# Causal attention and MLP: four heads at a time in 32-row and 32-column TensorE tiles, turns on VectorE, and one list schedule for all engines

## The chip, the core and the metric

The kernel runs on one core of a Trainium2 chip. The metric is device microseconds of one execution, here 478.67 (median of 3, 476.93 to 481.06). The profile of one execution spans 474.5 us from its first to its last instruction.

The engines are named as in the profile: PE (TensorE, matrix products), PEld (its weight loads), DVE (VectorE), ACT (ScalarE), POOL (GpSimd), SP (SyncE, which here only starts transfers).

## The reference

Attention over 8 batches of 8 heads, 576 queries of width 64, with 16 "beacon" keys ahead of 576 causal ones; then an MLP with a gated activation over all 4608 tokens.

```python
B, H, S, Nb, D = (8, 8, 576, 16, 64)
k_all = np.concatenate([beacon_k, k], axis=2)
v_all = np.concatenate([beacon_v, v], axis=2)
scores = scale * np.matmul(q, k_all.transpose(0, 1, 3, 2))      # scale = 1/8
causal[:, Nb:] = np.triu(np.ones((S, S), dtype=bool), k=1)
scores = np.where(causal, -1000000000.0, scores)
scores = scores - scores.max(-1, keepdims=True)
a = np.exp(scores)
a /= a.sum(-1, keepdims=True) + 1e-09
attn = np.matmul(a, v_all)
# ---- MLP, d_model 512, d_ff 2048 ----
x = attn.transpose(0, 2, 1, 3).reshape(B * S, H * D)
h = x @ w_in
g = h * (1.0 / (1.0 + np.exp(-1.702 * h)))
return (g @ w_out).astype(np.float32)
```

All inputs and the output are float32; both kernels multiply in float16.

## The kernel before

Attention goes by head pairs: 32 steps of two heads (NPAIR = 4 pairs a batch). q and k are loaded with the token on the partition, and turned by TensorE against an identity, then copied out of PSUM by ScalarE (q) and VectorE (k):

```python
def tr_pair(b, p, which):
    ...
        for i in range(NSB):                       # NSB = 5 row blocks; batch 0 has a form of its own
            rows = min(P, S - i * P)
            nc.tensor.transpose(
                u[:, i * P : i * P + rows],
                src[0:rows, i, 2 * p : 2 * p + 2, :].rearrange("r h d -> r (h d)"),
                ident[0:rows, 0:rows],
            )
    ...
    if which == 0:
        nc.scalar.copy(out=dst, in_=srcv)
    else:
        nc.vector.tensor_copy(out=dst, in_=srcv)
```

Scores are made with keys on the partition, in four chunks a pair, each head in one 64-row half of the array; exp goes from PSUM to SBUF, and the diagonal blocks are masked by VectorE (first 8 pairs) or GpSimd:

```python
def qk_chunk(i, ci):
    ...
    sc = pss.tile([P, 2, 512], F32, tag="s", name="s")          # pss: 2 buffers
    for (j, a, e) in CH[ci]:
        for x in range(2):
            r = 64 * x
            nc.tensor.matmul(sc[:, x, o : o + e - a],
                kT[r : r + 64, p, j * P : (j + 1) * P], qT[r : r + 64, p, a:e], start=True, stop=True)
    nc.scalar.activation(out=E[...], in_=sc[:, :, 0:o], func=AFT.Exp, scale=0.125)
    ...                                                          # mask of diagonal blocks
```

Values carry 64 columns of ones beside the 64 of v, so that the sums come out of the same matmul. The result is copied to SBUF; the sums are gathered by DMA, inverted, sent to DRAM and spread back over the partitions; GpSimd multiplies:

```python
def av_half(i, x, half):
    u = psu.tile([P, HS], F32, tag="u", name="u")                # psu: 3 buffers
    ...  nc.tensor.matmul(u[:, lo - qa : hi - qa], lhs, E[0:kw, x, col : col + hi - lo], ...)
    nc.vector.tensor_copy(out=O[:, p % 2, qa:qe], in_=u[:, :])

def z_gather(b, hf):   # SP: zc <- O, two transfers
def z_recip(b, hf):    # DVE: rc = 1 / zc;  SP: zd (DRAM) <- rc;  SP: rz <- zd, broadcast over 64 rows
def norm(b, hf):       # POOL: xT = O * rz, four multiplies of [64, 576]
```

The MLP goes in nine groups of 512 tokens. The first layer's four matmuls fill a bank, ScalarE makes the tanh and VectorE the gate; the second layer collects 16 matmuls in one bank (pso: 1 buffer), which ScalarE copies out:

```python
def mlp1(g, nt):
    u = psu.tile([P, GT], F32, tag="u", name="u")
    ...  nc.tensor.matmul(u[:, o : o + w], w1t[:, kp, nt * P : (nt + 1) * P], xT[:, kp, m : m + w], ...)
    nc.scalar.activation(out=sig[:, :], in_=u[:, :], func=AFT.Tanh, scale=0.851)
    nc.vector.scalar_tensor_tensor(out=gts[g][:, nt, :], in0=sig[:, :], scalar=1.0, in1=u[:, :],
                                   op0=ALU.add, op1=ALU.mult)

def mlp2(g, mt, qt):
    for nt in range(4 * qt, 4 * qt + 4):
        nc.tensor.matmul(o[:, :], gts[g][:, nt, mt * P : (mt + 1) * P], w2t[:, nt, :], ...)
    if qt == 3:
        nc.scalar.mul(out=osb[:, :], in_=o[:, :], mul=0.5)
        nc.sync.dma_start(out=out[t0 : t0 + P, :], in_=osb[:, :])
```

The order is fixed by hand: each step's attention pieces are spread over the step, and up to eight MLP pieces (`QUOTA = 8`) are put between them. A group of the MLP is begun when the whole batches that it needs are normalised. Loads start in the order: q and k of two head pairs at a time, v, then w1, then batch 1.

Of the kernel before, what the change touches and what calls it, by code (L numbers as in the profile page):

```python
# [11 lines left out]
ALU = mybir.AluOpType  # L13


@with_exitstack
def kernel(
# [19 lines left out]
    P = 128  # L37
    NJ = (NK + P - 1) // P
    NSB = (S + P - 1) // P
    NKPAD = NJ * P  # L40
    NPAIR = H // 2
    NKP = DMODEL // P
    NNT = DFF // P
    TR = 6
    TP = S // TR
    HS = S // 2
    GT = 512
    NG = NTOK // GT
    RING = 4
    NSTEP = B * NPAIR  # L50
    QUOTA = 8
    LAG = 6
# [4 lines left out]
    ld = ctx.enter_context(tc.tile_pool(name="ld", bufs=2))  # L57
    tp = ctx.enter_context(tc.tile_pool(name="tp", bufs=2))
    ep = ctx.enter_context(tc.tile_pool(name="ep", bufs=2))
    op_ = ctx.enter_context(tc.tile_pool(name="op", bufs=2))  # L60
# [3 lines left out]
    pss = ctx.enter_context(tc.tile_pool(name="pss", bufs=2, space=bass.MemoryType.PSUM))  # L64
    psu = ctx.enter_context(tc.tile_pool(name="psu", bufs=3, space=bass.MemoryType.PSUM))
    pso = ctx.enter_context(tc.tile_pool(name="pso", bufs=1, space=bass.MemoryType.PSUM))
    dr = ctx.enter_context(tc.tile_pool(name="dr", bufs=4, space=bass.MemoryType.DRAM))


    ident = cst.tile([P, P], F16, tag="ident", name="ident")  # L70
    make_identity(nc, ident)

    keep = cst.tile([P, P + Nb], F16, tag="keep", name="keep")
# [7 lines left out]
        pattern=[[1, P + Nb]],  # L81
        channel_multiplier=-1,
    )
    w1t = cst.tile([P, NKP, DFF], F16, tag="w1", name="w1")
    w2t = cst.tile([P, NNT, DMODEL], F16, tag="w2", name="w2")
    xT = cst.tile([P, NKP, RING * S], F16, tag="xT", name="xT")

    vbs = [cst.tile([P, NJ, H, 2 * D], F16, tag=f"vb{i}", name=f"vb{i}") for i in range(2)]
    for t in vbs:
        nc.vector.memset(t[:, :, :, D : 2 * D], 1.0)  # L90


    nat = {}

    def new_nat(b):

        shape = [TP, H, TR * D] if b == 0 else [P, NSB, H, D]
        qn = ld.tile(shape, F16, tag="qn", name="qn")
        kn = ld.tile(shape, F16, tag="kn", name="kn")
        bk = ld.tile([Nb, H, D], F16, tag="bk", name="bk")  # L100
        nat[b] = (qn, kn, bk)

    def load_qk(b, h0, h1):
        qn, kn, _ = nat[b]
        for t, src in ((qn, q), (kn, k)):
            if b == 0:
                nc.gpsimd.dma_start(
                    out=t[:, h0:h1, :],
                    in_=src[b, h0:h1].rearrange("h (p t) d -> p h (t d)", t=TR),
                )  # L110
                continue
            for i in range(NSB):
                rows = min(P, S - i * P)
                nc.gpsimd.dma_start(  # L114
                    out=t[0:rows, i, h0:h1, :],
                    in_=src[b, h0:h1, i * P : i * P + rows, :].rearrange("h s d -> s h d"),
                )

    def load_bk(b):
        nc.gpsimd.dma_start(out=nat[b][2][:, :, :], in_=beacon_k[b].rearrange("h n d -> n h d"))  # L120

    def load_v(b, j, h0, h1):
        vb = vbs[b % 2]
        if j == 0:
            nc.gpsimd.dma_start(
                out=vb[0:Nb, 0, h0:h1, 0:D],
                in_=beacon_v[b, h0:h1].rearrange("h n d -> n h d"),
            )
            nc.gpsimd.dma_start(
                out=vb[Nb:P, 0, h0:h1, 0:D],  # L130
                in_=v[b, h0:h1, 0 : P - Nb, :].rearrange("h n d -> n h d"),
            )
        else:
            lo = j * P - Nb
            hi = min(lo + P, S)
            nc.gpsimd.dma_start(  # L136
                out=vb[0 : hi - lo, j, h0:h1, 0:D],
                in_=v[b, h0:h1, lo:hi, :].rearrange("h n d -> n h d"),
            )

    def load_w1(c):
        w = DFF // 4
        nc.gpsimd.dma_start(
            out=w1t[:, :, c * w : (c + 1) * w],
            in_=moe_w_in[:, c * w : (c + 1) * w].rearrange("(a p) n -> p a n", p=P),
        )

    def load_w2(c):
        n = NNT // 4
        nc.gpsimd.dma_start(  # L150
            out=w2t[:, c * n : (c + 1) * n, :],
            in_=moe_w_out[c * n * P : (c + 1) * n * P, :].rearrange("(a p) n -> p a n", p=P),
        )


    qk = {}

    def new_qk(b):
        qT = tp.tile([P, NPAIR, S], F16, tag="qT", name="qT")
        kT = tp.tile([P, NPAIR, NKPAD], F16, tag="kT", name="kT")  # L160
        nc.gpsimd.memset(kT[:, :, NK:NKPAD], 0.0)
        qk[b] = (qT, kT)

    def tr_beacon(b):
        bk, kT = nat[b][2], qk[b][1]
        u = psu.tile([P, NPAIR, Nb], F16, tag="u", name="u")
        for p in range(NPAIR):
            nc.tensor.transpose(u[:, p, :], bk[:, 2 * p : 2 * p + 2, :], ident[0:Nb, 0:Nb])  # L168
        nc.vector.tensor_copy(out=kT[:, :, 0:Nb], in_=u[:, :, :])

    def tr_pair(b, p, which):
        src = nat[b][which]
        dst = qk[b][0][:, p, :] if which == 0 else qk[b][1][:, p, Nb:NK]
        if b == 0:
            u = psu.tile([P, TR, TP], F16, tag="u", name="u")
            for t in range(TR):
                for x in range(2):
                    nc.tensor.transpose(
                        u[64 * x : 64 * x + 64, t, :],
                        src[:, 2 * p + x, t * D : (t + 1) * D],  # L180
                        ident[0:TP, 0:TP],
                    )
            dst = dst.rearrange("r (p t) -> r p t", t=TR)
            srcv = u[:, :, :].rearrange("r t p -> r p t")
        else:
            u = psu.tile([P, S], F16, tag="u", name="u")
            for i in range(NSB):
                rows = min(P, S - i * P)
                nc.tensor.transpose(  # L189
                    u[:, i * P : i * P + rows],  # L190
                    src[0:rows, i, 2 * p : 2 * p + 2, :].rearrange("r h d -> r (h d)"),
                    ident[0:rows, 0:rows],
                )
            srcv = u[:, :]
        if which == 0:
            nc.scalar.copy(out=dst, in_=srcv)  # L196
        else:
            nc.vector.tensor_copy(out=dst, in_=srcv)  # L198


    s0s = [max(0, j * P - Nb) for j in range(NJ)]


    CH = [
        [(0, 0, 512)],
        [(0, 512, S), (2, s0s[2], S), (4, s0s[4], S)],
        [(1, s0s[1], S)],
        [(3, s0s[3], S)],
    ]
    ecol = {}  # L210
    choff = []
    c0 = 0
    for ch in CH:
        choff.append(c0)
        for (j, a, e) in ch:
            ecol[(j, a)] = c0
            c0 += e - a
    ETOT = c0
    Es = {}

    def e_pieces(j, a, e):

        got = []
        for (jj, qa), col in ecol.items():
            if jj != j:
                continue
            qe = qa + [x[2] - x[1] for ch in CH for x in ch if x[0] == jj and x[1] == qa][0]
            lo, hi = max(a, qa), min(e, qe)
            if lo < hi:
                got.append((lo, hi, col + lo - qa))  # L230
        return got

    def qk_chunk(i, ci):
        b, p = divmod(i, NPAIR)
        qT, kT = qk[b]
        if ci == 0:
            Es[i] = ep.tile([P, 2, ETOT], F16, tag="E", name="E")
        E = Es[i]
        sc = pss.tile([P, 2, 512], F32, tag="s", name="s")
        o = 0  # L240
        for (j, a, e) in CH[ci]:
            for x in range(2):
                r = 64 * x
                nc.tensor.matmul(  # L244
                    sc[:, x, o : o + e - a],
                    kT[r : r + 64, p, j * P : (j + 1) * P],
                    qT[r : r + 64, p, a:e],
                    start=True,
                    stop=True,
                )  # L250
            o += e - a
        nc.scalar.activation(  # L252
            out=E[:, :, choff[ci] : choff[ci] + o],
            in_=sc[:, :, 0:o],
# [3 lines left out]
        for (j, a, e) in CH[ci]:  # L258
            if a != s0s[j]:
                continue  # L260
            w = P - Nb if j == 0 else min(P, S - a)
            mc = Nb if j == 0 else 0
            col = ecol[(j, a)]
            blk = E[:, :, col : col + w]
            if i < 8:
                for x in range(2):
                    nc.vector.tensor_tensor(  # L267
# [178 lines left out]
    for p in range(NPAIR):  # L446
        load_qk(0, 2 * p, 2 * p + 2)
        if p == 0:
            load_bk(0)
# [102 lines left out]
```

The softmax here doesn't subtract the row's maximum and nothing guards it: scores larger than these inputs give would overflow.

## Time and profile before

| what | value |
|---|---|
| time | 478.67 us |
| span in the profile | 474.5 us |
| mean granted TensorE clock | 0.941 |
| first matmul of the MLP's first layer (line 382) | 89.8 us |
| last score matmul (line 244) | 378.8 us |
| small packets (under 512 B) | 109696 of 122016 |

The profile gives busy time and share of the span for each engine, and then the span in 40 equal slices of 11.9 us, with one digit for the busy tenths of each. Matmuls are pipelined, so that the mean duration of one is longer than the distance from one to the next. A line such as `L382 PE MATMUL u<-xT,w 128*128 128x512 f16 x512 | busy, mean | idle <- releaser` names the line of the kernel, the engine and operation, what is written and read, rows and columns of the array, the moving operand, the count, the busy microseconds, the mean nanoseconds of one, and the idle time of the engine just before, with what ended it. In the chain of waits, one goes back from the last instruction to what released it, step by step.

### The profile page before, as it was taken

How to read it: one execution, taken by the hardware profiler on the slowest of the kernel's cores; microseconds unless marked ns; L12 is line 12 of the kernel's file. 1: busy time of each engine (PE TensorE's matmuls, PEld its weight loads, DVE VectorE, ACT ScalarE, POOL GpSimd, SP SyncE). 2: the span in 40 equal slices, each digit the busy share in tenths (PEclk: the TensorE clock that was granted, in tenths of full speed). 3: DMA queues.
4: the chain of work that ended last, by engine and by line, in shares of the span. 5: the costliest groups of instructions: out<-in, count | busy, mean ns of one | idle time of the engine just before them, and what ended most of it. 6: DMA issues, size and time to landing. Idle time of an engine off the chain costs nothing.

```text
span 474.5 us, 6853 instructions
## 1 busy us (share of the span) xinstructions
PE 396.0 (83%) x2584; PEld 201.8 (43%) x2584; DVE 193.0 (41%) x410; ACT 222.8 (47%) x341; POOL 251.3 (53%) x348
## 2 busy tenths in 40 slices
PE   2505555889999999899989998999899999899985
PEld 1303333444444444444444456645444444444432
DVE  5403373755125522561256226622561373184410
ACT  3303433665456545664466446644665442263421
POOL 9945078489528952895379627954616250400000
PEclk9955675899999999999999999999999999999999
DMA  9999939959614981399129911990203112100111
GB/s 86 157 176 179 82 46 148 79 44 111 111 59 56 111 122 46 65 107 129 47 55 110 134 48 52 108 140 34 63 2 95 56 42 64 77 1 22 46 44 66
DMA packets 122016, 38.22 MB, mean 81 GB/s; under 512 B 109696, under 2 KB 115328, under 8 KB 121984
## 3 DMA queue, kind: packets, MB, share of 16 engines
q0 software_dynamic: 111424, 18.62, 54.9%
q1 hardware_dynamic: 10560, 19.18, 14.2%
q8 instruction: 20, 0.33, 0.3%
q14 instruction: 12, 0.10, 0.1%
HBM read 46.66 MB, written 9.58 MB: 119 GB/s over the span
## 4 chain that ended last, share of the span: by engine, by line
PE 59%; ACT 17%; POOL 7%; DMA 7%; DVE 5%; issue 4%; ACTq 0%; POOLq 0%; DVEq 0%
PE o L408 26%; PE u L382 19%; ACT E L252 8%; PE u L310 6%; ACT sig L391 5%; PE u L189 4%; DVE g L392 4%; PE s L244 3%; ACT osb L417 3%; DMA w<-in_moe_w_in_dram 3%; DMA bk<-in_beacon_k_dram 2%; POOL kn L114 1%; POOL vb L136 1%; DMA zc<-O 1%; POOL xT L354 1%
## 5 line engine op out<-in xcount | busy, mean ns | idle before, releaser
L382 PE MATMUL u<-xT,w 128*128 128x512 f16 (+1 forms) x640 | 144.7, 358 | 12.5 <-DVE g L392 12.4
L408 PE MATMUL o<-w,g 128*128 128x512 f16 x576 | 144.1, 379 | 9.7 <-ACT osb L417 9.7
L392 DVE SCALAR_TENSOR_TENSOR g<-sig,u 128x512 f16<-128x512 f16 x144 | 99.0, 687 | 104.9 <-ACT sig L391 104.8
L354 POOL TENSOR_TENSOR xT<-O,rz 64x576 f16<-64x576 f32 x64 | 89.6, 1400 | 79.9 <-DMA rz<-zd 76.3
L391 ACT ACTIVATE sig<-u 128x512 f16<-128x512 f32 x144 | 87.6, 609 | 77.3 <-PE u L382 72.9
L252 ACT ACTIVATE E<-s 128x1024 f16<-128x1024 f32 (+3 forms) x128 | 104.7, 876 | 14.8 <-PE s L244 8.8
L317 DVE COPY O<-u 128x288 f32<-128x288 f32 x128 | 56.3, 453 | 71.2 <-PE u L310 69.9
L382 PEld LDWEIGHTS <-w 128*128 128x128 f16 x640 | 56.8, 97 | 63.3 <-issue 20.4
L274 POOL TENSOR_SCALAR_AFFINE_SELECT E<-E 128x256 f16<-128x256 f16 (+2 forms) x120 | 43.1, 395 | 67.0 <-ACT E L252 66.3
L408 PEld LDWEIGHTS <-g 128*128 128x128 f16 x576 | 50.2, 97 | 63.1 <-issue 15.6
L310 PE MATMUL u<-E,vb 128*128 128x288 f16 (+6 forms) x576 | 69.5, 260 | 5.3 <-DVE O L317 5.1
L310 PEld LDWEIGHTS <-vb 128*128 128x128 f16 (+1 forms) x576 | 52.5, 104 | 36.8 <-issue 12.2
L417 ACT ACTIVATE osb<-o 128x512 f32<-128x512 f32 x36 | 21.5, 597 | 82.1 <-PE o L408 82.1
L244 PE MATMUL s<-qT,kT 64*128 64x80 f16 (+5 forms) x384 | 44.1, 307 | 18.4 <-ACT E L252 9.9
L196 ACT COPY qT<-u 128x576 f16<-128x576 f16 x32 | 20.5, 640 | 73.4 <-PE u L189 66.7
L244 PEld LDWEIGHTS <-kT 64*128 64x128 f16 x384 | 17.1, 99 | 58.6 <-issue 46.2
L114 POOL DMA_DIRECT2D kn<-in_k_dram x35 | 29.6, 883 | 5.9 <-DMA w<-in_moe_w_in_dram 5.9
L136 POOL DMA_DIRECT2D vb<-in_v_dram x36 | 29.7, 860 | 2.7 <-DMA w<-in_moe_w_out_dram 2.7
L198 DVE COPY kT<-u 128x576 f16<-128x576 f16 x32 | 15.7, 492 | 37.2 <-PE u L189 35.6
L114 POOL DMA_DIRECT2D qn<-in_q_dram x35 | 29.9, 884 | 0.0
L168 PE MATMUL u<-ident,bk 16*128 16x16 f16 x32 | 2.1, 170 | 28.2 <-DMA bk<-in_beacon_k_dram 28.2
L267 DVE TENSOR_TENSOR E<-E,keep 128x128 f16<-128x128 f16 (+2 forms) x80 | 17.1, 271 | 14.0 <-ACT E L252 13.6
(29 smaller groups left out, 108.8 us busy)
## 6 DMA issues: line engine op xcount, KB each, us to landing
rz<-zd SPq DMA_DIRECT2D x32, 288.0 KB, 4.4
out_dram<-osb SPq DMA_DIRECT2D x36, 256.0 KB, 2.0
qn<-in_q_dram POOLq DMA_DIRECT2D x28, 128.0 KB, 4.2
kn<-in_k_dram POOLq DMA_DIRECT2D x28, 128.0 KB, 4.4
vb<-in_v_dram POOLq DMA_DIRECT2D x21, 128.0 KB, 6.0
w<-in_moe_w_in_dram POOLq DMA_DIRECT2D x4, 512.0 KB, 9.3
w<-in_moe_w_out_dram POOLq DMA_DIRECT2D x4, 512.0 KB, 9.5
vb<-in_v_dram POOLq DMA_DIRECT2D x7, 112.0 KB, 3.3
```

Source lines behind the costliest of these rows:

```text
L114: nc.gpsimd.dma_start(out=t[0:rows, i, h0:h1, :], in_=src[b, h0:h1, i * P : i * P + rows, :].rearrange("h s d -> s h d"),)
L244: nc.tensor.matmul(sc[:, x, o : o + e - a], kT[r : r + 64, p, j * P : (j + 1) * P], qT[r : r + 64, p, a:e], start=True, stop=True,)
L252: nc.scalar.activation(out=E[:, :, choff[ci] : choff[ci] + o], in_=sc[:, :, 0:o], func=AFT.Exp, scale=0.125,)
L274: nc.gpsimd.affine_select(out=blk, in_=blk, compare_op=ALU.is_ge, fill=0.0, base=mc, pattern=[[0, 2], [1, w]], channel_multiplier=-1,)
L310: nc.tensor.matmul(u[:, lo - qa : hi - qa], lhs, E[0:kw, x, col : col + hi - lo], start=(n == 0), stop=(n == len(mm) - 1),)
L317: nc.vector.tensor_copy(out=O[:, p % 2, qa:qe], in_=u[:, :])
L354: nc.gpsimd.tensor_tensor(out=xT[r : r + 64, p, c : c + S], in0=O[r : r + 64, a, :], in1=rz[r : r + 64, a, :], op=ALU.mult,)
L382: nc.tensor.matmul(u[:, o : o + w], w1t[:, kp, nt * P : (nt + 1) * P], xT[:, kp, m : m + w], start=(kp == 0), stop=(kp == NKP - 1),)
L391: nc.scalar.activation(out=sig[:, :], in_=u[:, :], func=AFT.Tanh, scale=0.851)
L392: nc.vector.scalar_tensor_tensor(out=gts[g][:, nt, :], in0=sig[:, :], scalar=1.0, in1=u[:, :], op0=ALU.add, op1=ALU.mult,)
L408: nc.tensor.matmul(o[:, :], gts[g][:, nt, mt * P : (mt + 1) * P], w2t[:, nt, :], start=(nt == 0), stop=(nt == NNT - 1),)
L417: nc.scalar.mul(out=osb[:, :], in_=o[:, :], mul=0.5)
```

## The change

The new kernel takes four heads (a "set") at a time, 16 sets in all, and replaces several parts:

- **Turning q and k.** They are loaded so that partition 32h + r holds 18 tokens of head h in one run. VectorE transposes 32 x 32 squares of four-byte words; a word is two neighbouring float16 values of a row. So partition 32h + c holds elements 2c and 2c+1 of head h, and the two are taken apart by a step of two in the matmul's operands. No transposes on TensorE are left.
- **Scores.** Each head has 32 rows of the array, four heads side by side, in two passes (`d` = 0, 1) that add up. One score buffer of four banks in place of two buffers of two.
- **Values and sums.** Four heads side by side in 32 columns each; three groups: the lower and the upper half of v's columns, and ones.
- **Normalisation.** VectorE alone: transpose of the sums, reciprocal of one column, transpose back over 32 columns, and one multiply out of PSUM into `xT`, which now holds all tokens.
- **PSUM.** Values, first layer and second layer share a ring of four single banks.
- **Order.** A list schedule made when the program is built: every operation has an engine, an assumed length and its dependencies, and the order on all engines is that of the starts in this plan. Attention of later sets is held to due times from 30 to 275 us of the plan.
- **Groups.** Tokens 0 to 511 make two groups of 256; a group needs only the half batches that it covers.
- **Loads.** w1 comes in 24 pieces (its rows follow the new order of `xT`'s partitions), after q and k of two sets and v of batch 0; w2 after them.

The diff, cut to its core:

```diff
-    QUOTA = 8
-    LAG = 6
+class Plan:
+    LAT = {"PE": 230, "ACT": 60, "DVE": 60, "POOL": 60, "Q": 1900, "SP": 0}
+    ...                                    # list schedule, one queue for each engine
+    def choose(self, ok, t, mode, last, free):
+        ...                                # scores first; values late or in the same tile mode; then m1 and m2 in turn
@@ loads and turns
-            t = ld.tile([P, NSB, H, D]) ...  src[b, h0:h1, i * P : i * P + rows, :].rearrange("h s d -> s h d")
+            out=dst[s % NB3][:, :],
+            in_=src[b, Q * hs : Q * hs + Q].rearrange("h (r t) d -> (h r) (t d)", t=TR),
-                nc.tensor.transpose(u[:, ...], src[...], ident[0:rows, 0:rows])
-            nc.scalar.copy(out=dst, in_=srcv)
-            nc.vector.tensor_copy(out=dst, in_=srcv)
+        nc.vector.transpose(
+            out=f32(dst.rearrange("p n e -> p (n e)")).rearrange("p (r t) -> p t r", t=TR),
+            in_=f32(src[:, :]).rearrange("p (t c) -> p t c", t=TR),
+        )
@@ scores
-    pss = ... bufs=2 ...  sc = pss.tile([P, 2, 512], F32)
+    pss = ... bufs=1 ...  sc = pss.tile([P, Q, 512], F32)
+    CH = [
+        [(0, 0, HF), (1, s0s[1], HF), (2, s0s[2], HF)],
+        [(0, HF, S), (4, s0s[4], S)],
+        [(2, HF, S), (3, s0s[3], s0s[4])],
+        [(3, s0s[4], S), (1, HF, S)],
+    ]
+            for d in range(2):
+                for h in range(Q):
+                    r = 32 * h
+                    nc.tensor.matmul(
+                        sc[:, h, o : o + e - a],
+                        kT[s % NB2][r : r + 32, j * P : (j + 1) * P, d],
+                        qT[s % NB2][r : r + 32, a:e, d],
+                        start=(d == 0),
+                        stop=(d == 1),
+                    )
@@ values and sums
+    def e_av(s, x, half):
+        u = ring_tile(("av", s, x, half))
+            for h in range(Q):
+                lhs = ones[0:kw, :] if x == 2 else vb[...][0:kw, j, Q * hs + h, HD * x : HD * x + HD]
+                nc.tensor.matmul(u[32 * h : 32 * h + 32, a - q0 : e - q0], lhs, E[0:kw, h, ...], ...)
-        nc.vector.tensor_copy(out=O[:, p % 2, qa:qe], in_=u[:, :])
@@ normalisation
-        zc <- O, zd <- rc, rz <- zd by DMA;  nc.gpsimd.tensor_tensor(xT, O, rz, mult)
+        nc.vector.transpose(out=zt[:, :], in_=rings[("av", s, 2, half)][:, 0:HF])
+        nc.vector.reciprocal(out=rc[:, :], in_=zt[...][:, :, 0])
+        nc.vector.transpose(out=rz[...], in_=rc[...].to_broadcast([P, HF // 32, 32]))
+        nc.vector.tensor_tensor(out=xT[...], in0=rings[("av", s, x, half)][:, 0:HF], in1=rz, op=ALU.mult)
@@ groups and order
+    GROUPS = [(0, 256), (256, 512)]        # then 512 each
+    T_ATT0, T_ATT1 = 30000, 275000
+    order = plan.run()
+    for o in order:
+        o.emit()
```

## Prediction

> **What bounds the kernel now.** I read the busy shares first, then the slices.
>
> ```profile
> PE 396.0 (83%) x2584; PEld 201.8 (43%) x2584; DVE 193.0 (41%) x410; ACT 222.8 (47%) x341; POOL 251.3 (53%) x348
> ...
> PE   2505555889999999899989998999899999899985
> ...
> PEclk9955675899999999999999999999999999999999
> ```
>
> TensorE is the only engine near full, but not in the first seven slices of 11.9 us: to about 88 us it is half idle and its clock is at half. After that it is full to the end. So there are two things to win: the start, and TensorE work per batch.
>
> The start is explained by the chain that ended last, here in order of time (start, length, what):
>
> ```profile
> 18.18 11.96 DMA w<-in_moe_w_in_dram
> ...
> 45.13 2.90 PE u L310 x18
> 48.54 5.64 DMA zc<-O
> 54.67 2.46 DMA zd<-rc
> 57.16 4.40 DMA rz<-zd
> 61.70 1.40 POOL xT L354
> ```
>
> The MLP may begin only when all of batch 0 is normalised; the sums go through three DMA trips (5.64 + 2.46 + 4.40 us) and four GpSimd multiplies, and head pairs 3 and 4 come after w1 and batch 1's q and k. The first MLP matmul starts at 89.8 us.
>
> The steady part, from the busy times of a stretch that is one batch long (columns: total, then each engine's busy time) and the groups by line and shape:
>
> ```profile
> 151.60:199.80 48.20, 44.53 (x293) 21.91 (x293) 19.90 (x39) 25.95 (x42) 32.50 (x47) 1.00 0.78 85
> ```
> ```profile
> L408 PE MATMUL o<-w,g 128*128 128x512 f16 x576 | 144.1, 379 | 9.7 <-ACT osb L417 9.7
> L382 PE MATMUL u<-xT,w 128*128 128x512 f16 x512 | 128.2, 379 | 10.6 <-DVE g L392 10.4
> ...
> L310 PE MATMUL u<-E,vb 128*128 128x288 f16 x192 | 48.2, 310 | 0.0
> ...
> L244 PE MATMUL s<-qT,kT 64*128 64x512 f16 x64 | 13.9, 427 | 6.7 <-DVE kT L198 6.7
> ```
>
> A batch takes 48.2 us. The 379 ns is a modelled latency, not a pace: in the chain, 68 first-layer matmuls take 14.68 us, so 216 ns each, 0.42 ns a column. A batch's MLP is 576 tokens, 144 matmuls' worth: 144 x 0.216 = 31.1 us. The other 17.1 us are attention and waits. From the distances between matmul starts in three batches (151.6 to 296.2): transposes 3.6 us a batch, scores 4.9, values with sums 9.5 (these hold some of the waits).
>
> Whether small tiles run side by side decides the case. The timeline shows batch 0's transposes, in two 64-column tiles side by side:
>
> ```profile
> 50.52 0.45 PE L178 MATMUL u<-ident,qn 96*64 96x96 f16 x12
> ...
> 50.75 0.33 PEld L178 LDWEIGHTS <-kn 96*64 96x64 f16 x12
> 50.80 0.42 PE L178 MATMUL u<-ident,kn 96*64 96x96 f16 x12
> ```
>
> Twelve matmuls, each with its own weights, start in 0.28 us (50.52 to 50.80): 23 ns each, where one 96-column stream alone is 40 ns. So two column tiles do overlap. Scores do too: the eight score matmuls at 61.52 last 0.62 us with the pipeline's latency, while their 1984 columns one after the other would be 0.83 us.
>
> **What the Trainium skill says.** "TensorEngine Tiling (Array Packing)", Key Properties: tiles load and multiply independently, but a change of tiling mode drains the engine. The trace agrees: tiles overlap as above, and from a 64-row score matmul to a full one I find about 0.1 us beyond the stream. "TensorE: Matmul & The Clock Gate", Measured speedup vs the span model, gives 3.07x for four row tiles and 2.38x for three column tiles of 512 columns; the trace has only two tiles at a time. "SBUF — State Buffer", Door 1, says that reads run at full rate with at least two hits in a 16-byte line; the new q and k are read with a four-byte step, four hits, so I take no loss. No strided operand in this trace shows it.
>
> **Part by part.**
>
> *Transposes on TensorE* go: 3.6 us a batch, and 20.5 + 15.7 us of evacuations on ScalarE and VectorE. Instead 32 VectorE turns of 576 words; a 512-wide VectorE instruction from the page is 687 ns, so about 0.8 us each, 26 us.
>
> *Scores.* D=64 is split in two passes of 32 rows, four heads at once. A set of four heads has nine pieces, 1664 columns; two passes. A group of four matmuls costs the greater of its stream and four times 23 ns = 92 ns. Four pieces of 288 columns (122 ns) and five short ones (92): 2 x (488 + 460) = 1.9 us, plus four blocks x 0.2 us for the mode change in and out = 2.7 us a set, 5.4 a batch against 4.9. No gain: rows are as full as before.
>
> *Values and sums.* Three groups (two halves of D, ones) in place of two heads x 128 columns: eight pieces, 4 x 122 + 4 x 92 = 0.86 us, x 3 = 2.6 us, with mode changes in perhaps four blocks x 0.2 = 3.4 us a set, 6.8 a batch against 9.5. A stream of 3 x 1664 instead of 4 x 1664 for four heads.
>
> Attention on TensorE is then 12.2 us a batch, MLP 31.1: 43.3 against 48.2, in all 8 x 4.9 = 39 us less. The second layer's waits for its single output bank (9.7 us in the group above, 0.69 us after each tile near the end) lie in the old 17.1; the ring of four banks should hide them, and I count them as part of the 4.9, not on top.
>
> *Normalisation* moves to VectorE out of PSUM: no O copy (56.3 us), no GpSimd multiply (89.6 us), no DRAM trip. Added: 64 multiplies of 288 at about 453 ns (like the O copy) = 29 us; 32 turns of sums at 0.45 = 14; 32 x (reciprocal 0.3 + turn 0.45) = 24.
> VectorE in all: gates 128 x 0.687 + 32 x 0.42 = 101, + 29 + 14 + 24 + 26 + first masks 5 = 200 us (193 before).
> ScalarE: exp from the two rows 1024 wide 1019 ns and 416 wide 549 ns: 0.77 ns an element + 227 ns, so 6656 elements and four instructions are 6.05 us a set, 97 in all; tanh 128 x 0.609 + 32 x 0.4 = 91; outputs 21.5: 209 us.
> GpSimd: masks 204 ns + 0.82 ns an element (rows 256 and 160 wide), 3.1 us a set x 14 = 44; about 110 issues at 0.55 to 0.85 = 80: 124 us, half of before. None of the three reaches 60% of the new span.
>
> *The start.* q and k are now 2304-byte runs and come first; the first q in the old trace lands 3.2 us after issue, so q and k of set 0 are in by 7.5 us, turned by 8.7. With one score buffer, scores and exp alternate: four times (0.8 + 0.2 + 1.5) at half clock, 10 us a set; set 1's first chunk is exponentiated by 22 us, sums, turn, reciprocal, turn and norm take about 4 us: first MLP group (256 tokens, half of batch 0) at 27 us. w1: 14 issues before it to 10 us, its 24 issues by 24 us; in the old trace a quarter of w1 lands every 2.5 us, 10 us in all, so the first part is there in time. w2 follows at about 33 us and lands by 45 us; the 14 us of first-layer work of 512 tokens and attention fill that.
>
> Sum: 27 us to the first MLP matmul, holding batch 0's attention (12.2); then 8 x 43.3 - 12.2 = 334; last evacuation and store 3: 364. The times are some 4 us above the traced span (478.7 against 474.5): 368. For waits that the new single order does not foresee I add 8 us: **376 us**.
>
> **Rivals.**
> 1. *The four tiles do not overlap.* Then scores are 8 x 1664 columns a set = 5.5 us and values 12 x 1664 = 8.3; with mode changes 15.4 us against my 6.1, x 16 = +149 us: about 525, slower. For it: no 32-wide tile in the trace, shorter columns, and a weight load ahead of every one of them. Against it: the 23 ns pace. Two at a time (scores 2.8, values 4.2, changes 1.6: 8.6 us a set) would give +40, 416.
> 2. *The ring of four banks becomes the wait.* First-layer tiles hold a bank for matmul, tanh and gate (0.86 + 0.2 + 0.61 + 0.69, some 2.6 to 3 us with queueing), values for sums, two turns and norm, second-layer tiles 4 to 7 us. I get some 950 bank-us, 240 of 370 us per bank: two thirds. Like before's ring (12.4 us of waits for the gate, 9.7 for the output). If VectorE's turns and ScalarE's 1.8 us exps come in the way at bad times: +30 us, 405.
> 3. *The start stays long*, because w1 in 24 pieces or the masks and turns on VectorE come late: first MLP at 45 instead of 27: 394. Before has such waits (issues stalled 5.9 us for a w1 landing).
>
> **Range and chances.** The pace of tiles and the start are read from the trace, so I put 0.75 on the overlap holding nearly as computed; half overlap still wins. Waits only add; a lower end comes from fewer mode changes. Range 352 to 412. Faster 0.94, same 0.02, slower 0.04.
>
> **What would show it.** First MLP matmul near 27 us and clock at full from 30 us; score groups of four starting within about 100 ns, value groups of 288 every 122 ns; 43 us of TensorE a batch; no transposes; VectorE near 200 us, GpSimd near 125; value-tile waits for VectorE below 25 us. Wrong if short matmuls start over 40 ns apart, if mode changes cost far above 0.1 us, or if "TensorE waits for the gate or the norm" leads the waits.

## Result and the profile after

The changed kernel takes 364.34 us (363.99 to 364.56), the one before 479.0 beside it: ratio 0.761, interval 0.757 to 0.765. The traced span went from 474.5 to 362.6 us. The prediction was 376, range 352 to 412.

Busy time and slices of the changed kernel, the same view as before (a slice is now 9.1 us):

```profile
PE 332.7 (92%) x3904; PEld 169.8 (47%) x3904; DVE 202.7 (56%) x385; ACT 203.7 (56%) x261; POOL 114.4 (32%) x200
...
PE   0168888999999999999999999999999999999995
...
PEclk9999999999999999999999999999999999999999
```

The span less PE's busy time gives the first account: busy 396.0 to 332.7 us (63.3 less), not busy 78.5 to 29.9 us (48.6 less), together the 111.9 us of the span. So both of the things to be won were won: less TensorE work, and a start that fills sooner. From the eighth slice to the last but one TensorE is never below nine tenths, and the clock on record is never at half (there is no record of it before 29.3 us).

The steady stretch, and the waits in it (first view: stretch, then busy time of each engine; second: who waited for whom, microseconds in all, times, longest):

```profile
151.60:199.80 48.20, 48.02 (x660) 23.98 (x659) 31.58 (x59) 31.44 (x38) 19.61 (x32) 1.00 0.61 81
```
```profile
POOL E L389 <- ACT E L361: 147.7, 34, 11.3
...
PE s L350 <- DVE kT L335: 15.6, 3, 14.9
...
PE s L350 <- ACT E L361: 5.8, 5, 2.0
...
PE u L461 <- DVE g L481: 2.3, 6, 0.8
...
PE u L461 <- DVE xT L442: 1.2, 3, 0.7
```

In 48.2 us TensorE is busy for 48.02, where it had 44.53. Its longest wait is a single one, 14.9 us before the first score matmul. GpSimd's 147.7 us lead the list and cost nothing: that engine is free for two thirds of the time. The waits for gates fell from 12.4 us to 2.3, those for the output bank (9.7) are gone.

The groups that the prediction spoke of (total and mean of one, idle before):

```profile
L350 PE MATMUL s<-qT,kT 32*128 32x288 f16 (+4 forms) x1152 | 37.3, 251 | 21.6 <-DVE kT L335 15.6
...
L335 DVE STREAM_TRANSPOSE kT<-kn 128x576 f32<-128x576 f32 x16 | 20.1, 1257 | 0.5
L335 DVE STREAM_TRANSPOSE qT<-qn 128x576 f32<-128x576 f32 x16 | 19.9, 1244 | 0.0
```

A turn is 1.25 us, not 0.8. And the chain that ended last begins with a transfer that the prediction did not put on the path (start, length, what):

```profile
3.44 8.10 DMA bkf<-in_beacon_k_dram
```

Those are the beacon keys. VectorE's cast of them waits until they have landed, and the turns and the first scores stand behind it:

```profile
11.66 0.69 DVE L318 CAST bkn<-bkf 128x1024 f16<-128x1024 f32 x1 [9.50 <-DMA bkf<-in_beacon_k_dram]
...
14.89 1.04 PE L350 MATMUL s<-qT,kT 32*128 32x288 f16 x24 [14.89 <-DVE kT L335]
...
31.58 0.39 PE L461 MATMUL u<-xT,w 128*128 128x256 f16 x2
```

The distances between matmul starts, from the first to the last of a block (medians over the sets), give what one set costs TensorE without the changes of mode: scores 0.461, 0.320, 0.337 and 0.227 us for the four chunks, 1.35 in all (the expectations below count 1.42, with 0.320 for each of the last three); values and sums 0.667 us for the first half and 1.471 for the second, 2.14. First scores start at 14.9 us, the first MLP matmul at 31.6, the second layer at 60.5.

TensorE's busy time can also be split by kind of work: each busy stretch goes to the kind of matmul whose block started last.

| TensorE busy, us | before | change |
|---|---|---|
| transposes | 32.8 | 0 |
| scores | 39.2 | 33.2 |
| values and sums | 60.7 | 42.3 |
| MLP, both layers | 263.3 | 257.2 |

### The profile page after: what moved, and what is told of

Read it like the earlier page. It is cut to its first block, busy times and chain, and to the rows that moved or that the text cites. A ratio compares the mean times of both kernels' runs of the same rounds, so it can differ in the third digit from the quotient of the medians.

```text
span 362.6 us, 9064 instructions
## 1 busy us (share of the span) xinstructions
PE 332.7 (92%) x3904; PEld 169.8 (47%) x3904; DVE 202.7 (56%) x385; ACT 203.7 (56%) x261; POOL 114.4 (32%) x200
## 4 chain that ended last, share of the span: by engine, by line
PE 82%; DVE 8%; ACT 4%; DMA 2%; issue 1%; SPq 0%; DVEq 0%; ACTq 0%
PE u L493 34%; PE u L461 32%; PE u L413 9%; PE s L350 8%; ACT E L361 3%; DVE g L481 3%; DMA bkf<-in_beacon_k_dram 2%; DVE kT L335 2%; ACT sig L475 1%; DVE qT L335 1%; DVE xT L442 1%; DVE zt L424 0%; DVE rz L433 0%; SPq L233 0%; DVE bkf L207 0%
## 5 line engine op out<-in xcount | busy, mean ns | idle before, releaser
L481 DVE SCALAR_TENSOR_TENSOR g<-sig,u 128x512 f16<-128x512 f16 (+1 forms) x160 | 99.0, 630 | 98.4 <-ACT sig L475 97.9
L493 PE MATMUL u<-w,g 128*128 128x512 f16 x576 | 142.4, 379 | 0.0
L475 ACT ACTIVATE sig<-u 128x512 f16<-128x512 f32 (+1 forms) x160 | 87.5, 554 | 84.6 <-PE u L461 80.3
L361 ACT ACTIVATE E<-s 128x2048 f16<-128x2048 f32 (+1 forms) x64 | 99.6, 1556 | 47.3 <-PE s L350 46.7
L389 POOL TENSOR_SCALAR_AFFINE_SELECT E<-E 128x448 f16<-128x448 f16 (+2 forms) x84 | 42.4, 530 | 147.7 <-ACT E L361 147.7
L350 PE MATMUL s<-qT,kT 32*128 32x288 f16 (+4 forms) x1152 | 37.3, 251 | 21.6 <-DVE kT L335 15.6
L350 PEld LDWEIGHTS <-kT 32*128 32x128 f16 x1152 | 22.8, 96 | 47.1 <-issue 27.2
L413 PE MATMUL u<-E,vb 128*32 128x288 f16 (+4 forms) x1024 | 31.5, 260 | 0.3 <-DVE zt L424 0.3
L442 DVE TENSOR_TENSOR xT<-u,rz 128x288 f16<-128x288 f32 x64 | 26.4, 451 | 3.5 <-PE u L413 0.8
L424 DVE STREAM_TRANSPOSE zt<-u 128x288 f32<-128x288 f32 x32 | 15.3, 479 | 22.4 <-PE u L413 22.3
L413 PEld LDWEIGHTS <-vb 128*32 128x32 f16 (+1 forms) x1024 | 22.7, 98 | 6.4 <-issue 3.4
L413 PE MATMUL u<-E,ones 128*32 128x288 f16 (+4 forms) x512 | 18.3, 263 | 0.6 <-ACT E L361 0.3
L433 DVE STREAM_TRANSPOSE rz<-rc 128x288 f32<-128x288 f32 x32 | 15.3, 478 | 1.1
```

The costliest lines, as they stand in the source:

```text
L350: nc.tensor.matmul(sc[:, h, o : o + e - a], kT[s % NB2][r : r + 32, j * P : (j + 1) * P, d], qT[s % NB2][r : r + 32, a:e, d], start=(d == ...
L361: nc.scalar.activation(out=Es[s][:, :, base[c] : base[c] + w], in_=ss[(s, c)][:, :, 0:w], func=AFT.Exp, scale=0.125,)
L389: nc.gpsimd.affine_select(out=blk, in_=blk, compare_op=ALU.is_ge, fill=0.0, base=off + (Nb if j == 0 else 0), pattern=[[0, Q], [1, w]], ch ...
L413: nc.tensor.matmul(u[32 * h : 32 * h + 32, a - q0 : e - q0], lhs, E[0:kw, h, col : col + e - a], start=(i == 0), stop=(i == n - 1),)
L442: nc.vector.tensor_tensor(out=xT[:, 2 * hs + x, t0 : t0 + HF], in0=rings[("av", s, x, half)][:, 0:HF], in1=zs[(s, half)][1][:, :], op=ALU. ...
L475: nc.scalar.activation(out=sig[:, 0:w], in_=rings[("m1", g, nt)][:, 0:w], func=AFT.Tanh, scale=0.851)
```

## Experiments

**TensorE as the bound.** The score passes are done twice:

```diff
-            for d in range(2):
+            for d in (0, 1, 0, 1):
```

> Every score matmul is run twice (the second pair of passes overwrites the first). Theory (TensorE is the bound from about 60 us on, so what is added to it is paid in full): the score passes are 1.42 us a set by their starts, 14 of 16 sets lie after 40 us: +20 to +23 us, about 386. Rival (the chain of scores, exp, masks and turns paces the sets, and TensorE has slack): +5 us or less, 369.

Measured 388.87 us, +24.5. Its busy line:

```profile
PE 356.9 (92%) x5056; PEld 191.1 (49%) x5056; DVE 203.4 (52%) x385; ACT 206.1 (53%) x261; POOL 114.4 (30%) x200
```

TensorE is busy 24.2 us longer, and the time grew by just that; the time not busy stayed (387.5 - 356.9 = 30.6 against 29.9). TensorE work that is added is paid in full, slightly more than the 20 to 23 us of the theory. By the starts a set's scores grew from 1.35 to 2.83 us, some 24 for 16 sets; in the split of the busy time they grew by 25.2 (33.2 to 58.4).

**Do the tiles overlap?** First the two loops were swapped, so that each head's matmuls stand together:

```diff
-            for d in range(2):
-                for h in range(Q):
+            for h in range(Q):
+                for d in range(2):
...
-        for i, (j, a, e) in enumerate(AVP[half]):
-            for h in range(Q):
+        for h in range(Q):
+            for i, (j, a, e) in enumerate(AVP[half]):
```

> The two loops around the score and value matmuls are swapped: all matmuls of one head, then of the next, so that neighbours stand in the same tile and only the last of one head can overlap the first of the next. Same matmuls, same order of everything else. Theory (tiles side by side make attention cheap on TensorE): a set's scores stream 5 x 1664 columns instead of 2 x 1664 (3.5 against 1.4 us), its values and sums about 18800 instead of 4992 (7.8 against 2.1 us), in all some 7.5 us a set, 16 sets: 364 + 120 = about 480. Rival (the gain comes from the order of work and from the transposes that are gone, the overlap is hidden by waits): under 385.

Measured 373.53 us, +9.2: far from my 480. Taken alone this would speak for the rival. But the expectation rested on an assumption of mine, that matmuls start in the order of the program. The timeline of this kernel refutes it (start, length, matmuls of one kind run together):

```profile
108.54 0.83 PE L413 MATMUL u<-E,ones 128*32 128x288 f16 x14
109.09 0.30 PE L413 MATMUL u<-E,vb 128*32 128x288 f16 x1
109.14 0.35 PE L413 MATMUL u<-E,ones 80*32 80x80 f16 x3
109.22 0.30 PE L413 MATMUL u<-E,vb 128*32 128x288 f16 x2
109.28 0.30 PE L413 MATMUL u<-E,ones 80*32 80x80 f16 x2
109.35 0.32 PE L413 MATMUL u<-E,vb 128*32 128x288 f16 x3
109.42 0.20 PE L413 MATMUL u<-E,ones 80*32 80x80 f16 x1
```

In the program all twenty matmuls with ones stand before the first one with vb. On the chip, the first of them starts at 109.09, when six of the twenty have not started; the last of those starts at 109.42. In this trace the tiles run as queues of their own, some way ahead of each other, so the swap removed little of the overlap: the long value block went from 1.471 to 1.996 us, the score chunks from 0.461 to 0.471. 16 x 0.525 = 8.4 us is nearly all of the 9.2. "TensorE: Matmul & The Clock Gate", The mechanism, has matmuls start in strict program order; between column tiles, this trace does not.

So overlap had to be taken away by the tile, not the order. All heads' scores from the first 32 rows (the other heads' scores are left out):

```diff
-                    r = 32 * h
+                    r = 0
```

> All four heads of a set take their score operands from rows 0 to 31, so that every score matmul stands in the same row tile (the other three heads' scores are left out: head 0's are computed four times). Same count, widths and order. Theory (four row tiles run side by side, and that keeps the scores cheap): 8 x 1664 columns one after the other, 5.5 us a set instead of 1.42, 16 sets: +60 to +66 us, 424 to 430. Rival (matmuls follow at a fixed pace of issue, whatever their tile, and swapping the loops cost little for that reason): under 372.

Measured 452.68 us, +88. A first chunk, in this kernel and then in the unaltered change:

```profile
149.77 2.02 PE L350 MATMUL s<-qT,kT 32*128 32x288 f16 x24
151.71 0.68 PE L413 MATMUL u<-E,ones 128*32 128x288 f16 x20
```
```profile
121.78 0.64 PE L350 MATMUL s<-qT,kT 32*128 32x288 f16 x24
122.35 0.68 PE L413 MATMUL u<-E,ones 128*32 128x288 f16 x20
```

The same 24 matmuls take 1.94 us (149.77 to 151.71) in one tile and 0.57 in four. By the starts, a set's scores are 1.83 + 1.30 + 1.45 + 1.20 = 5.78 us, so 16 x 4.43 = 71 us; the expectation of 60 to 66 took the stream alone. The trace shows where the other 17 are. In the split of the busy time scores grew by 82.8 us (33.2 to 116.0), everything else on TensorE by 8.4, and the time not busy fell by 2.9. Two stretches ran slower than the medians: the first two sets, until about 51 us, at half pace (288 columns every 240 ns, later every 127), and those from 77.1 to 97.5 us, where the clock on record is at half. The unaltered change has no such stretch after 29.3 us. What made the clock fall there is not shown.

And all values and sums in the first 32 columns, one head after the other (the heads overwrite each other, and the normalisation and the MLP's input hold 32 rows of values, the rest zeros):

```diff
-                    u[32 * h : 32 * h + 32, a - q0 : e - q0],
+                    u[0:32, a - q0 : e - q0],
```

> All four heads' values and sums go into columns 0 to 31, one head after the other (each overwrites the one before; the normalisation works on 32 partitions alone, at the same length of instruction; the MLP's other rows are zeros). Theory (four column tiles run side by side): 12 x 1664 columns one after the other, 8.3 us a set instead of 2.14, 16 sets: about +99 us, 455 to 465. Rival (fixed pace of issue): under 375.

Measured 461.6 us, +97. The first half of a set, 36 matmuls, and the block that follows it:

```profile
143.80 1.06 PE L414 MATMUL u<-E,ones 128*32 128x288 f16 x12
144.71 1.94 PE L414 MATMUL u<-E,vb 128*32 128x288 f16 x24
146.58 1.04 PE L494 MATMUL u<-w,g 128*128 128x512 f16 x4
```

By the starts a set's values are 2.67 + 5.93 = 8.6 us instead of 2.14: 16 x 6.46 = 103. TensorE's busy time grew by 101.1 us and the time not busy fell by 3.1, which leaves the 98 of the span. Both tile experiments fell on the side of the overlap. Without it in both places, the two additions of 88 and 97 us would bring the kernel to about 550 (an estimate, if they add up), slower than before.

**The early start.** The MLP may begin only after batch 2, as late as before:

```diff
-        return 0 if s < HS else T_ATT0 + T_CH * (4 * (s - HS) + c)
+        return 0 if s < 3 * HS else T_ATT0 + T_CH * (4 * (s - HS) + c)
...
+        if g < 2:
+            xs += [norms[(3 * HS - 1, x, h)] for x in range(2) for h in range(2)]
...
-        while g < NG and GROUPS[g][1] <= (b + 1) * S:
+        while b > 1 and g < NG and GROUPS[g][1] <= (b + 1) * S:
```

> The MLP may begin only after batch 2 is normalised (six sets, held to no due time), about where the kernel before began it (89.8 us). Theory (the early MLP fills TensorE while exp paces the first sets, and that is worth the idle time that it fills): six sets at some 11 to 12 us each end at 80 to 85 us with some 27 us of TensorE work in them, so idle grows from 26 to about 53 us: 388 to 394. Rival (the early MLP is only moved work, the late sets' slack takes it up): under 372.

Measured 390.3 us, +26.

```profile
PE 341.9 (88%) x3904; PEld 178.9 (46%) x3904; DVE 206.3 (53%) x385; ACT 206.1 (53%) x261; POOL 114.5 (29%) x200
...
PE   0265277669999999999999999999999999999996
...
PEclk9998656668999999999999999999999999999999
```

The MLP starts at 87.0 us here. The theory's number came out, but it is made of two parts: 17.9 us more not busy (389.7 - 341.9 = 47.8 against 29.9), and 9.2 us more busy with the same matmuls, which the theory did not have: in the thin slices the granted clock is at half for 41 of the 61 us from 28.2 to 89.6 (it is on record from 28.2 on). The kernel before shows the same: at half for 55 of the 65 us from 22.9 to 87.8. So that the theory's number came out is partly luck.

**Half groups.** One first group of 512 tokens:

```diff
-    GROUPS = [(0, 256), (256, 512)]
+    GROUPS = [(0, 512)]
```

> The first 512 tokens make one group instead of two of 256, so the MLP begins when all of batch 0 is normalised, not half of it. Theory (the early MLP fills idle time): first MLP matmul some 4 to 6 us later, but 256-wide gates and tanhs cost VectorE and ScalarE 16 extra instructions each, which fall away: between 363 and 368. Rival (half groups are what makes the start): 370 or more.

Measured 365.63 us (364.45 to 366.76), +1.3, within the theory's 363 to 368; its fastest runs are no slower than the 364.34 of the change, so the difference is hardly clear of noise. The first MLP matmul comes at 37.6 us, 6.0 later. The start needs the MLP early, but half a batch earlier is worth little or nothing.

**The ring.** Three banks in place of four:

```diff
-    RING = 4
+    RING = 3
```

> Three banks in the ring of values, first and second layer instead of four. Theory (with four banks the ring is not the bound; in the changed kernel TensorE waits 2.3 us for gates and 1.2 for norms): a quarter of the banks gone brings waits, but not many, +6 to +12 us, about 373. Rival 2 of the prediction (the ring is at its limit): +25 us or more, 390.

Measured 374.7 us, +10.4: the theory's number, but only in part its waits. The time not busy grew by 4.3 us (372.9 - 338.7 = 34.2); the other 6.0 are busy time, in an order that has 52 blocks of values instead of 41. With four the ring is not the bound; with one bank fewer it begins to be. Five were not tried.

**The turn.** Squares written side by side (the tokens' right order is left out):

```diff
-            out=f32(dst...).rearrange("p (r t) -> p t r", t=TR),
+            out=f32(dst...).rearrange("p (t r) -> p t r", t=TR),
```

> The turns of q and k write their squares one after the other instead of with a step of 18 words (the tokens then stand in another order, so the causal mask does not fit them: this leaves out the right order). Theory (the step of 72 bytes in the writes is what makes a turn 1.25 us, against 0.48 us for 288 words): a turn at 0.75 to 0.8 us, VectorE 15 us less busy; TensorE is the bound after 60 us, so only the start gains: 362 to 363.5. Rival (VectorE's load shapes the waits all through): 358 or less.

Measured 361.75 us, -2.6. The two groups:

```profile
L335 DVE STREAM_TRANSPOSE kT<-kn 128x576 f32<-128x576 f32 x16 | 12.5, 778 | 0.6
L335 DVE STREAM_TRANSPOSE qT<-qn 128x576 f32<-128x576 f32 x16 | 12.2, 763 | 0.0
```

0.77 us instead of 1.25: the step of 72 bytes in the write costs 0.48 us a turn. The 15 us taken from the turns (VectorE's busy time falls from 202.7 to 190.2) are worth 2.6, slightly more than the 0.8 to 2.3 of the theory and far from the rival's 6; first scores start at 14.1 and the first MLP matmul at 30.6, 1.0 us earlier. VectorE is not the bound.

**The first wait.** Beacons of batch 0 first:

```diff
-            out=bkf[32 * a : 32 * a + Nb, :, :],
-            in_=beacon_k[:, a::Q, :, :].rearrange("b g n d -> n (b g) d"),
+            out=bkf[32 * a : 32 * a + Nb, 0:HS, :],
+            in_=beacon_k[0:1, a::Q, :, :].rearrange("b g n d -> n (b g) d"),
+            ...                                  # then beacon_k[1:B] into HS:NSET, cast apart; bkf is zeroed in two parts
```

> The beacon keys of batch 0 are loaded in four small transfers ahead of those of the other batches, and cast apart; in the changed kernel the first turn waits for all of them until 11.5 us, with q and k landed at 8.0. Theory (the start is a chain: load, turn, scores, exp): first scores at about 9.5 instead of 14.9 us, first MLP at about 26.5 instead of 31.6, and the end 3 to 5 us earlier: 360. Rival (w1 and w2 pace the first 60 us): first scores earlier, the end within 1 us of 364.

Measured 359.16 us, -5.2. In its start the cast waits 4.33 us, not 9.50. The transfers start at 1.10 us instead of 2.03, as there is less to zero before them. q and k of set 0 land at 6.2 and 7.8 us, and their turns now start soon after that:

```profile
6.50 0.23 DVE L324 CAST bkn<-bkf 128x128 f16<-128x128 f32 x1 [4.33 <-DMA bkf<-in_beacon_k_dram]
6.64 1.25 DVE L341 STREAM_TRANSPOSE qT<-qn 128x576 f32<-128x576 f32 x1
...
9.26 1.04 PE L356 MATMUL s<-qT,kT 32*128 32x288 f16 x24 [9.26 <-DVE kT L341]
```

First scores 5.6 us earlier, end 5.2 us earlier: the start is a chain, and almost all of it is paid.

**A better version.** On top of that, a plan with measured lengths and other due times:

```diff
-    T_ATT0, T_ATT1 = 30000, 275000
+    T_ATT0, T_ATT1 = 26000, 265000
-                "DVE", 760 + 100 * which,
+                "DVE", 1250 + 200 * which,
-                    1700, 3 * (c1 - c0) // 2
+                    1300, 3 * (c1 - c0) // 2
```

> The split beacon load (359.2), and a plan with lengths nearer the measured ones (a turn 1.25 us instead of 0.76, a pair of w1 issues 1.3 instead of 1.7) and due times from 26 to 265 us instead of 30 to 275. Theory (only the first 60 us still have idle TensorE time, some 10 us between matmuls and 9.5 before the first): 1 to 3 us less, 356 to 358. Rival (the order is already as good as its inputs allow, or a new order brings waits later): 359 to 361.

Measured 355.07 us (ratio to before 0.742, interval 0.739 to 0.744): 4.1 less than the split load and 1 below the expected range, better than both kernels.

```profile
PE 330.6 (94%) x3904; PEld 169.7 (48%) x3904; DVE 203.7 (58%) x387; ACT 204.4 (58%) x261; POOL 114.3 (32%) x200
```

Not busy is down to 22.7 us, 9.2 of them before the first matmul. How much of the 4.1 belongs to the lengths and how much to the due times is open; they were not tried apart.

## Why the prediction was right, step by step

*The tiles overlap (rival 1 falls).* Right, and shown by taking the tile away: +88 and +97 us.

*The pace of short matmuls* was mis-sized. I took 23 ns a matmul as an issue pace and so 92 ns as the least for a group of four. But the two 64-column tiles that I read it from were bound by their stream: two streams of 96 columns in 42 ns. The real floor is lower. In the changed kernel four matmuls start within some 10 ns; four of 80 columns follow the last four after 39 ns and four of 48 columns after 26 (medians). So scores are 1.35 us a set (about 1.6, an estimate, with the 0.42 ns a column of each chunk's last matmuls) where I had 1.9, values 2.14 where I had 2.6. With mode changes, the score and value starts of the stretch 60 to 280 us, up to the start of what follows them, give 1.94 and 2.52 us a set, and the entries another 0.1 us a block: 2.3 + 2.8 = 5.1 against my 6.1. A batch is then 10.2 + 31.1 = 41.3 us, not 43.3. The 0.1 us for a mode change was right.

*The start* was too short: 31.6 us to the first MLP matmul, not 27. The step that failed is "q and k of set 0 are in by 7.5 us, turned by 8.7": q and k landed at 6.4 and 8.0, but the turn on VectorE stood behind the beacons' cast, and the last of their four transfers landed at 11.5. Also, a turn is 1.25 us. So the first scores came at 14.9 us, 6.2 later than I had them. The rest of the start was 1.6 us shorter: 16.7 us from there to the first MLP matmul, where I had 18.3. The half clock that I had for the first sets was right, whatever the clock line shows for the time before its first record at 29.3 us. The first chunk of set 1 takes 0.98 us up to the next block, against 0.57 for the one at 121.78 shown above:

```profile
25.88 1.04 PE L350 MATMUL s<-qT,kT 32*128 32x288 f16 x24
...
26.86 2.11 PE L413 MATMUL u<-E,vb 128*32 128x288 f16 x40
```

A set took 11.0 us (14.89 to 25.88), where I had 10. What was shorter is the end of the chain: from the exp of that chunk, done at 28.9, to the first MLP matmul it was 2.7 us, not 5.

*The sum again with measured terms:* 31.6 + 8 x 41.3 - 10.2 + 3.7 at the end + 5.9 of gaps after the first MLP matmul = 361.4, against a span of 362.6. (The 10.2 is slightly too much: 2.0 us of batch 0's attention come after the first MLP matmul.) The changes to my sum: start +4.6, attention -14, end +0.7, waits -2.1, and time above the span 1.7 instead of 4. They add up to -13; measured is -11.7. So the number came out 3% too high because a start taken too short and an attention taken too long partly cancel, which is luck; the overlap of the tiles, on which the gain rests, was right.

*Engines.* VectorE 202.7 (I had 200), ScalarE 203.7 (209), GpSimd 114.4 (124). In VectorE, turns 40.0 instead of 26, sums and back 37.4 (15.3 + 6.8 + 15.3) for 38, gates 99.1 for 101. That VectorE's total is so close is partly luck: its turns are 14 us longer than I had them, and its groups add up to some 212 us, of which 9 overlap in the profile and count once. Rival 2 falls, four banks suffice; rival 3, the long start, came true in small part: 4.6 of its 18 us, for another reason than those it named.

*Where the 111.9 us of span went.* Of the 63.3 us of busy time, 32.8 are the transposes, 6.0 the scores, 18.4 values and sums, 6.1 the MLP (the table above). Not all of it is less work: the kernel before is busy for 26.5 us while its clock is on record at half, the changed kernel for none, so some 13 us of the 63 are the clock (an estimate, half of the 26.5). No run put the transposes back by themselves. Of the 48.6 us not busy, 27.4 lie before the first MLP matmul (47.6 to 20.2), 20.9 after it (26.8 to 5.9), the rest at the end. The late-MLP run brings back 23.4 of the 27.4 and has 5.5 less after, the 17.9 in all. The 20.9 are the old steady waits, for gate and output bank above all.

## What to carry over

Where TensorE is full, count its stream in tiles: operands of 32 rows, or outputs of 32 columns, can share the array four at a time. Here 24.2 us more of TensorE's busy time cost 24.5 us, one for one, while mode changes of 0.1 us a side are cheap beside MLP pieces of 0.86. Look for what starts the chain, too: a small transfer that nobody counts, here 16 rows of beacons, was worth 5 us. And before a pace is read as a floor, ask whether its stream bounds it.

## What was not expected of the hardware

- Matmuls in different column tiles start out of program order, even across operations (109.09 against 109.42 us above).
- The least distance is one of a tile. In one row tile (all scores in one tile), matmuls of 48 columns follow every 25 ns, which agrees with the floor of about 25 ns that "TensorE: Matmul & The Clock Gate", Wait — 56ns, not 53.3ns?, gives; in four tiles, four of them follow every 26 ns, 6.5 ns each.
- A VectorE transpose of 576 words is 0.77 us with its squares packed and 1.25 us with a step of 72 bytes in the write; reading q and k with a step of four bytes costs little, as I had assumed: in one row tile the next matmul follows 288 such columns after 127 ns, in one column tile it follows 288 packed ones of the values after 122 ns. With four tiles the second pass of 288 starts 140 ns after the first (128 where the passes are done twice), values 124.
